# A state-space convolution and a routed expert layer on one core: the convolution's pieces issued in another order up to the second block of scores

## The chip, the core and the metric

The kernel runs on one core of a Trainium2 chip. The core has a matrix engine (TensorE: PE, its weight loads PEld), a vector engine (DVE), an activation engine (ACT), GpSimd (POOL) and a sync engine (SP), on which this kernel issues all its DMAs. Each engine works through its instructions in the order in which they were issued. The metric is the device time of one execution in microseconds, the median of several runs.

## What is computed

Two layers, each behind a layer norm and added to its input; 2048 positions, 512 channels. Cut to what matters:

```python
x = A_u
h = x + conv(layernorm(x))
out = h + peer(layernorm(h))

def conv(u):                       # S4D: a long convolution for each channel
    dt = exp(log_dt); A = -exp(log_A_real) + 1j * A_imag
    C = (C_real + 1j * C_imag) * dt[:, None]
    K = 2 * einsum("dn,dnl->dl", C, exp((A * dt[:, None])[:, :, None] * pos)).real
    return irfft(rfft(u, 2 * L) * rfft(K, 2 * L), 2 * L)[:L] + u * D_skip

def peer(x):                       # 32 heads, 2 x 16 keys, 256 experts
    q = einsum("nd,dhc->nhc", x, w_q)
    i1 = argmax(q[..., :128] @ k1.T); i2 = argmax(q[..., 128:] @ k2.T)
    e = 16 * i1 + i2               # one expert for each head
    act = gelu(einsum("nd,nhd->nh", x, u[e]))
    return einsum("nh,nhd->nd", act, v[e])
```

## The kernel before

The kernel doesn't issue its work where it describes it. It describes 1729 pieces (`plan.add`, line 134: an engine, a function, what it reads, writes and takes), and at the end `plan.run(ORDER)` (line 155) calls their functions in the order of a tuple of numbers, `ORDER` (line 34). The order only decides which instruction stands ahead of which on each engine's queue. What an instruction waits for follows from what it reads and writes, and from the buffers that it takes: seven banks of PSUM shared by nearly all products of the convolution, and rings of two for most tiles in SBUF. A transfer on SP is also a piece of the order, and one that has to wait holds up all transfers behind it. Numbers are given as a piece is described: 0 to 16 are loads, 17 to 64 the parameters, 66 to 112 and 984 to 1102 the projection's pieces, 181 onward the convolution.

The pieces that the order moves:

- **Loads** (line 271): the SSM's parameters (ldt, lar, aim, cre, cim), the keys ka and kb, the input x in eight transfers for the statistics (two tiles, x_105 and x_106 in the rows below), small constants.
- **Parameters** (lines 293 to 436): chains of small operations on ACT and DVE that make the decays' exponents, the roots (lines 332 to 334), angles (line 355, 340 to 342) and magnitudes, for a first part (64 states' columns, 0) and the rest (1). `decays` (line 373) makes eleven powers of the decay with exp: E for the first half of the channels (two calls, 64 and 192 columns), and e1 for the second half (256 columns), which is stored to memory and read back much later (E<-e_d).
- **Projection pieces** (`w_piece(n)`, line 799, n = 0 to 31): w_q times keys is computed on the chip. Each piece is a load of 512 KB (line 822), 16 matmuls (line 828), a copy (832), a transpose (836) and a copy (840); every fourth one is followed by a store to w_d (844). The loads of pieces 2 to 8 go to tiles that are used for something else later (pb, e1, c_s). From piece 11 on each shares a ring of two tiles: its load waits until the matmuls of the piece before the last are through.
- **Statistics and norm** (lines 230 to 262): 64 bn_stats on DVE, then a mean on PE, spread on DVE, square on ACT, parts on DVE, variance on PE, square root on ACT, reciprocal on DVE.
- **The convolution kernel's generation**, 32 rounds i, the heart of the first half: POOL builds magnitudes mg and phases pg (`factors`, lines 538 to 594), ACT the sines and cosines (lines 644 to 647), DVE multiplies (`tables`, lines 651 to 664), PE contracts (`kgen`, line 690: 64 matmuls). mg, pg and the products gf are rings of two. Two rounds give a k tile, copied by ACT and DVE (lines 698 and 702).
- **The transform**, four column blocks c: stage 1 of the normalised input (s1u, line 471, behind the load, subtraction and product of lines 502 to 508) and of k (s1k), stage 2 (line 488), their products (lines 732 to 743, DVE, ACT and POOL), and the first inverse stage (ia, line 764), whose results go to memory. Behind block 3 come the inverse (ib, line 1036), the second norm, scores, selection and experts. That second half starts at about 300 us.

ACT's functions come from tables: where the next one isn't in the table at hand, an ACT_TABLE_LOAD stands ahead. Exp, square root, and sine with arctangent are three tables here.

Of the kernel before, what the change touches and what calls it, by code (L numbers as in the profile page):

```python
# [27 lines left out]
def view(t, off, dims):  # L28
# [6 lines left out]
    0, 18, 19, 2, 5, 1, 4, 71, 3, 66, 87, 11, 76, 81, 92, 17, 20, 21, 22, 6, 24, 25, 23, 27, 30, 26, 29, 35, 36, 37,  # L35
    97, 38, 40, 41, 67, 68, 32, 31, 39, 33, 42, 61, 72, 73, 43, 34, 62, 44, 45, 47, 123, 28, 48, 69, 70, 181, 77, 78,
    74, 46, 54, 79, 55, 88, 89, 82, 83, 80, 84, 93, 94, 95, 102, 8, 75, 984, 59, 90, 98, 91, 108, 49, 64, 56, 184, 99,
    186, 103, 50, 104, 14, 122, 51, 52, 248, 185, 245, 187, 53, 182, 183, 197, 198, 96, 105, 188, 106, 190, 85, 189,
    192, 194, 200, 191, 249, 193, 202, 195, 201, 63, 100, 109, 196, 110, 199, 12, 86, 989, 101, 128, 204, 206, 111,
    203, 215, 129, 207, 205, 112, 57, 58, 208, 218, 220, 222, 985, 986, 987, 990, 216, 217, 988, 209, 16, 991, 992,  # L40
    13, 126, 7, 994, 10, 1000, 227, 228, 246, 116, 229, 387, 993, 219, 125, 124, 995, 996, 224, 230, 997, 998, 127,
    221, 1005, 210, 223, 225, 231, 114, 247, 120, 65, 1001, 1002, 226, 232, 107, 234, 144, 236, 1006, 1010, 211, 212,
    233, 213, 1007, 1003, 1011, 235, 9, 250, 237, 238, 252, 214, 1012, 1004, 239, 1008, 1013, 1015, 117, 1021, 137,
    1009, 254, 256, 121, 115, 240, 118, 119, 253, 243, 1016, 130, 131, 244, 1014, 257, 258, 132, 1017, 1018, 1019,
    388, 261, 262, 251, 264, 266, 133, 138, 1022, 1023, 390, 134, 135, 1026, 1027, 255, 259, 999, 151, 145, 136, 146,
    260, 1028, 1029, 1024, 263, 279, 280, 139, 267, 281, 265, 268, 269, 1030, 147, 1025, 270, 142, 140, 271, 152, 291,
    153, 241, 148, 143, 282, 141, 284, 286, 283, 149, 272, 292, 154, 113, 150, 242, 156, 273, 274, 158, 288, 294, 157,
    155, 159, 285, 160, 277, 289, 1020, 278, 391, 287, 275, 276, 295, 161, 163, 296, 290, 162, 293, 389, 392, 393,
    164, 298, 165, 343, 344, 177, 167, 175, 345, 166, 297, 1031, 299, 300, 394, 301, 302, 168, 357, 178, 358, 359,
    350, 351, 352, 176, 396, 303, 179, 180, 398, 400, 304, 395, 399, 403, 397, 401, 169, 307, 60, 305, 171, 173, 308,  # L50
    306, 319, 406, 408, 404, 407, 170, 174, 454, 172, 348, 346, 320, 349, 405, 421, 410, 402, 422, 423, 1032, 360,
    409, 411, 347, 15, 412, 424, 1033, 413, 433, 362, 1036, 1037, 455, 361, 414, 426, 363, 1038, 1034, 1035, 364, 311,
    434, 315, 451, 415, 428, 425, 1042, 1039, 1040, 593, 1041, 365, 427, 416, 366, 312, 429, 353, 354, 430, 1043,
    1044, 355, 356, 369, 431, 370, 436, 435, 452, 367, 368, 316, 1045, 323, 385, 386, 377, 378, 1047, 1048, 432, 1049,
    437, 438, 324, 440, 549, 563, 439, 550, 317, 318, 551, 1046, 321, 1050, 1051, 371, 372, 373, 374, 379, 313, 322,
    442, 380, 441, 1052, 383, 443, 594, 314, 384, 381, 375, 309, 310, 596, 444, 382, 456, 453, 457, 467, 376, 468,
    458, 460, 459, 462, 552, 597, 553, 554, 463, 555, 570, 339, 464, 335, 340, 445, 461, 331, 465, 470, 446, 472, 474,
    336, 471, 469, 485, 476, 466, 486, 556, 327, 473, 1057, 475, 488, 490, 477, 497, 478, 557, 492, 558, 489, 493,
    325, 337, 328, 333, 479, 480, 487, 491, 332, 571, 494, 498, 500, 326, 564, 338, 502, 504, 506, 495, 501, 598, 499,
    503, 595, 334, 565, 329, 330, 496, 599, 417, 419, 601, 603, 507, 505, 610, 605, 420, 447, 448, 600, 508, 481, 449,  # L60
    611, 612, 418, 661, 602, 606, 509, 510, 607, 604, 608, 513, 483, 511, 609, 450, 482, 613, 484, 514, 572, 658, 629,
    512, 527, 614, 615, 616, 617, 521, 528, 619, 618, 529, 620, 559, 560, 568, 1053, 1054, 522, 621, 569, 1058, 622,
    1059, 517, 530, 623, 1060, 1061, 561, 1055, 575, 573, 566, 518, 562, 628, 631, 632, 633, 641, 576, 635, 574, 630,
    634, 519, 523, 567, 579, 637, 580, 589, 1056, 640, 643, 642, 1063, 756, 770, 1068, 636, 520, 591, 644, 590, 638,
    577, 585, 524, 586, 662, 525, 645, 578, 1064, 646, 639, 647, 1065, 592, 583, 584, 581, 659, 803, 515, 526, 648,
    649, 650, 516, 660, 1066, 1067, 1069, 587, 1070, 1071, 663, 674, 1072, 763, 665, 667, 651, 652, 653, 669, 342,
    341, 1078, 675, 582, 666, 664, 531, 532, 539, 757, 758, 537, 670, 676, 668, 671, 677, 588, 540, 679, 681, 672,
    764, 678, 545, 682, 546, 800, 1073, 683, 680, 684, 673, 759, 761, 685, 538, 692, 695, 697, 699, 686, 693, 694,
    533, 696, 760, 543, 535, 687, 700, 698, 701, 702, 762, 777, 704, 705, 801, 707, 708, 706, 778, 779, 544, 802, 709,
    711, 712, 534, 710, 771, 713, 714, 541, 542, 703, 690, 765, 624, 626, 688, 715, 656, 805, 804, 806, 691, 536, 807,  # L70
    808, 625, 627, 809, 811, 716, 717, 812, 654, 689, 813, 657, 720, 721, 718, 1079, 719, 816, 819, 768, 772, 1080,
    810, 814, 655, 821, 823, 817, 820, 818, 822, 864, 1074, 724, 1075, 726, 1081, 725, 722, 723, 734, 735, 1076, 769,
    1077, 780, 1082, 782, 781, 825, 773, 774, 766, 775, 767, 1084, 1085, 1086, 824, 834, 867, 826, 815, 837, 730, 835,
    727, 731, 836, 1089, 736, 868, 776, 827, 783, 788, 798, 839, 840, 737, 732, 733, 828, 789, 1094, 841, 799, 728,
    729, 790, 791, 786, 787, 838, 796, 797, 784, 843, 794, 785, 795, 847, 548, 547, 742, 844, 865, 846, 848, 849, 744,
    842, 866, 851, 853, 855, 745, 829, 852, 845, 869, 870, 850, 1090, 752, 856, 854, 880, 857, 881, 1091, 871, 1083,
    1099, 873, 875, 872, 876, 753, 858, 748, 877, 743, 883, 749, 738, 874, 878, 898, 859, 885, 887, 1062, 1092, 884,
    792, 879, 793, 888, 889, 882, 886, 750, 890, 899, 740, 739, 910, 891, 1093, 901, 902, 903, 751, 905, 907, 746,
    741, 913, 747, 892, 906, 915, 900, 832, 833, 917, 919, 911, 904, 908, 893, 830, 831, 914, 912, 896, 916, 860, 861,
    862, 918, 909, 920, 921, 863, 922, 894, 897, 923, 926, 895, 927, 924, 925, 1087, 1088, 928, 929, 930, 932, 754,  # L80
    933, 1095, 936, 755, 934, 1096, 1097, 931, 940, 944, 1100, 948, 937, 938, 941, 942, 935, 945, 1098, 1101, 1102,
    952, 956, 939, 949, 943, 953, 946, 947, 950, 951, 954, 957, 958, 955, 1105, 1206, 959, 969, 1103, 1104, 963, 966,
    981, 1207, 1115, 964, 965, 970, 960, 975, 978, 972, 1112, 1119, 1109, 1106, 1120, 967, 1116, 1113, 982, 968, 1107,
    976, 961, 979, 973, 1110, 1121, 971, 1129, 1114, 983, 1108, 1117, 962, 977, 980, 974, 1111, 1130, 1131, 1122,
    1132, 1135, 1133, 1208, 1212, 1118, 1123, 1134, 1136, 1137, 1138, 1139, 1140, 1143, 1213, 1141, 1144, 1145, 1124,
    1214, 1146, 1125, 1126, 1142, 1147, 1281, 1209, 1152, 1210, 1353, 1153, 1163, 1154, 1148, 1149, 1150, 1211, 1215,
    1151, 1155, 1167, 1173, 1156, 1162, 1157, 1158, 1159, 1280, 1279, 1160, 1216, 1352, 1217, 1218, 1164, 1285, 1282,
    1165, 1176, 1283, 1286, 1219, 1166, 1284, 1220, 1161, 1287, 1168, 1169, 1170, 1221, 1354, 1225, 1222, 1288, 1171,
    1226, 1289, 1223, 1227, 1236, 1224, 1290, 1177, 1291, 1228, 1237, 1292, 1127, 1172, 1174, 1178, 1238, 1293, 1175,
    1179, 1184, 1182, 1183, 1239, 1185, 1128, 1294, 1295, 1180, 1186, 1181, 1230, 1231, 1232, 1229, 1309, 1241, 1242,  # L90
    1243, 1240, 1233, 1234, 1296, 1187, 1297, 1235, 1298, 1193, 1195, 1196, 1310, 1190, 1244, 1245, 1189, 1427, 1426,
# [1357 lines left out]
```

## Time and profile before

| | |
|---|---|
| time, median of 3 runs | 501.16 us (500.92 to 502.75) |
| the profiled execution | 502.31 us, span 500.5 us |
| granted clock, mean over the span | 0.988 |
| DMA | 61.04 MB, mean 122 GB/s |
| chain of work that ended last | PE 69%, DVE 19%, ACT 5%, issue 2%, DMA 2%, POOL 1% |

A row of the view of stretches gives, after the range and its length, the busy time of each engine with its count of instructions, the granted clock of TensorE, the DMA share, and GB/s. A row of the timeline gives start and length in us, engine, line, operation, out<-in, shapes, the count, and in brackets the idle time of the engine just ahead and what ended it. "issue" there is idle time for which the profile shows no cause. In the table of the chain it is time in which the engine waited for nothing that the profile shows. DMA rows name the issuing engine as SPq.

### The profile page before, as it was taken

The numbers are of one execution on the slowest core, as the hardware profiler recorded it, in microseconds if no ns is written. First come the engines' busy times: TensorE is split into PE (matmuls) and PEld (weight loads), VectorE is DVE, ScalarE is ACT, GpSimd is POOL, SyncE is SP. The second block draws the span as 40 slices with busy tenths as digits, with TensorE's granted clock in tenths as the row PEclk, the third lists the DMA queues.
The fourth block names the chain that finished last, engine by engine and source line by source line (L and its number), as shares of the span: only waits on it lengthen the run. The fifth ranks groups of instructions, "written<-read, shape, count | busy, mean of one in ns | idle before, by whom it ended". The sixth has DMA issues, their size and how long they took to land.

```text
span 500.5 us, 16696 instructions
## 1 busy us (share of the span) xinstructions
PE 448.6 (90%) x7206; PEld 393.6 (79%) x7206; DVE 408.5 (82%) x708; ACT 300.2 (60%) x596; POOL 325.0 (65%) x344
## 2 busy tenths in 40 slices
PE   0545879999999999999999689999999999999985
PEld 0324669989999989999998688887878888787874
DVE  4879998989988998799775494878979686978994
ACT  4796789986997689966996263454043430416231
POOL 3988997999999999989864303652263516535130
PEclk9999979999999999999999899999999999999999
DMA  7916885354200740045242757320171311010012
GB/s 259 413 52 211 275 297 173 145 156 195 65 3 9 266 131 24 3 102 218 64 162 72 227 158 251 110 103 1 61 226 54 117 56 44 1 45 0 1 51 78
DMA packets 27361, 61.04 MB, mean 122 GB/s; under 512 B 7028, under 2 KB 14456, under 8 KB 26136
## 3 DMA queue, kind: packets, MB, share of 16 engines
q1 hardware_dynamic: 27288, 59.98, 35.3%
q8 instruction: 56, 0.92, 0.8%
q14 instruction: 17, 0.14, 0.1%
HBM read 46.08 MB, written 13.89 MB: 120 GB/s over the span
## 4 chain that ended last, share of the span: by engine, by line
PE 69%; DVE 19%; ACT 5%; issue 2%; DMA 2%; POOL 1%; SPq 0%; ACTq 0%; DVEq 0%
PE sc L1150 14%; PE ia L764 12%; PE s1k L471 6%; PE kps L690 6%; PE s1u L471 5%; DVE oh L1280 5%; PE s2yu L488 5%; PE xu L1157 4%; PE s2yk L488 3%; PE ib L1036 3%; PE o L1327 2%; PE wps L828 2%; PE cnt L1290 2%; DVE U L733 2%; DMA wq<-wq 2%
## 5 line engine op out<-in xcount | busy, mean ns | idle before, releaser
L588 POOL TENSOR_TENSOR mg<-TS 128x1024 f32<-128x1024 f32 x32 | 62.7, 1958 | 11.4 <-PE kps L690 11.1
L557 POOL TENSOR_TENSOR pg<-PS 128x1024 int32<-128x1024 int32 x32 | 68.8, 2152 | 1.0 <-ACT t L644 0.9
L1280 DVE TENSOR_SCALAR oh<-idxb,ec_s 128x2048 bf16<-128x2048 bf16 (+1 forms) x72 | 50.3, 756 | 6.9 <-ACT idxb L1262 6.9
L764 PE MATMUL ia<-ca_s,U 128*128 128x128 f32 x256 | 50.6, 280 | 0.8 <-POOL U L743 0.8
L1192 POOL TENSOR_TENSOR ks<-kq 128x512 f32<-128x512 bf16 x16 | 17.3, 1079 | 49.0 <-DVE kq L1186 48.4
L1060 POOL TENSOR_TENSOR vs<-hc 128x256 f32<-128x256 f32 x8 | 6.3, 789 | 59.7 <-ACT hc L1083 59.7
L645 ACT ACTIVATE t<-t,halfpi 128x512 f32<-128x512 f32 x64 | 42.4, 662 | 2.1
L1150 PE MATMUL sc<-w_hi,hhi 128*128 128x480 f32 x128 | 42.5, 413 | 0.0
L764 PEld LDWEIGHTS ia<-ca_s,U 128*128 128x128 f32 x256 | 39.8, 196 | 1.0 <-POOL U L743 1.0
L644 ACT ACTIVATE t<-pg 128x512 f32<-128x512 int32 x64 | 38.9, 607 | 0.5 <-DVE U L735 0.4
L690 PE MATMUL kps<-mg 128*32 128x64 f32 x1024 | 34.6, 233 | 5.0 <-DVE mg L660 2.8
L764 PE MATMUL ia<-ca_s,yk 128*128 128x128 f32 x192 | 38.0, 280 | 0.6 <-DVE U L735 0.3
L1150 PE MATMUL sc<-w_hi,hlo 128*128 128x480 f32 x128 | 38.4, 381 | 0.0
L1150 PE MATMUL sc<-w_lo,hhi 128*128 128x480 f32 x128 | 38.4, 380 | 0.0
L647 ACT ACTIVATE t<-pg 128x512 f32<-128x512 int32 x64 | 37.9, 608 | 0.3 <-DVE gf L655 0.2
L594 POOL TENSOR_TENSOR mg<-TS 128x512 f32<-128x512 f32 x32 | 37.4, 1172 | 0.1
L690 PE MATMUL kps<-gf 128*32 128x64 f32 x1024 | 34.4, 231 | 0.6 <-issue 0.6
L690 PEld LDWEIGHTS kps<-mg 128*32 128x32 f32 x1024 | 26.0, 117 | 9.2 <-POOL mg L594 4.7
L471 PE MATMUL s1u<-c_s,xs 128*64 128x128 f32 x512 | 33.1, 285 | 0.0
L488 PE MATMUL s2yk<-yk,c_s 128*128 128x128 f32 x256 | 32.6, 279 | 0.4 <-ACT yk L474 0.4
L488 PE MATMUL s2yu<-yu,c_s 128*128 128x128 f32 x256 | 31.9, 279 | 0.1
L471 PE MATMUL s1k<-c_s,k 128*64 128x128 f32 x512 | 31.4, 279 | 0.5 <-DVE k L702 0.5
(200 smaller groups left out, 1385.2 us busy)
## 6 DMA issues: line engine op xcount, KB each, us to landing
wq<-wq SPq DMA_DIRECT2D x25, 512.0 KB, 4.6
t_d<-T SPq DMA_DIRECT2D x24, 256.0 KB, 4.5
Tb<-t_d SPq DMA_DIRECT2D x8, 768.0 KB, 6.6
x<-xa SPq DMA_DIRECT2D x8, 512.0 KB, 6.4
xs<-xb SPq DMA_DIRECT2D x16, 256.0 KB, 3.3
xt<-xt SPq DMA_DIRECT2D x8, 512.0 KB, 4.2
out<-ob SPq DMA_DIRECT2D x7, 512.0 KB, 3.0
c_s<-wq SPq DMA_DIRECT2D x4, 512.0 KB, 10.2
```

What stands on the lines that cost most here:

```text
L471: T.matmul(ps[64 * k:64 * k + 64, g, :], lhs8(4 * n + g), c1_s[:, k], start=True, stop=True)
L488: T.matmul(ps[:, k, :], c2_s[:, kk, :], y[:, :, kk, :], start=True, stop=True)
L557: G.tensor_tensor(view(pg, 0, [[32, 2 * NC], [8, 4], [1, 8]]), view(t["PS"], 1024 + off, [[1, 2 * NC], [128, 4], [0, 8]]), view(t["PS"], 8 ...
L588: G.tensor_tensor(view(mg, 0, [[96, NC], [8, 8], [1, 8]]), view(ts, 512 + 8 * o, [[8, NC], [1, 8], [0, 8]]), view(ts, 8 * o, [[8, NC], [0, ...
L594: G.tensor_tensor(view(mg, 64, [[96, NC], [8, 4], [1, 8]]), view(ts, 1536 + o, [[1, NC], [64, 4], [0, 8]]), view(ts, 1024 + 8 * o, [[8, NC ...
L644: A.activation(p, pg[:, :, k], AF.Abs)
L645: A.activation(p, p, AF.Sin, scale=-SINSCALE, bias=halfpi)
L647: A.activation(p, pg[:, :, k], AF.Sin, scale=SINSCALE)
L690: T.matmul(kps[32 * q:32 * q + 32, 2 * g + h, :], m[:, d, 64:96], m[:, d, 0:64], start=(e == 0), stop=(e == 1))
L764: T.matmul(ps[:, g, :], t[:, 4 * n + g].rearrange("p a b -> p (a b)"), ca_s[:, s, :], start=(s == 0), stop=(s == 1))
L1150: T.matmul(ps[:, 512 * h:512 * h + 480], t[x_][:, q, ts], I[w_][:, q, 480 * h:480 * h + 480], start=(q == 0 and x_ == w_), stop=(q == 3 an ...
L1280: V.tensor_scalar(oh[:, :, 0:ln], t["idxb"][:, :, sl], S["ec"][:, 4 * e + j:4 * e + j + 1], None, op0=ALU.is_equal)
```

## The change

The first 1199 numbers of `ORDER` stand in another order, found by a search with waits for instruction loads counted. They are all pieces of the convolution and of what stands ahead of it, up to the second block of scores; the 530 numbers behind are the same. No piece is added, dropped or altered. ACT has two fewer ACT_TABLE_LOADs, since the table is switched less often. The beginning of the tuple:

```diff
 ORDER = (
-    0, 18, 19, 2, 5, 1, 4, 71, 3, 66, 87, 11, 76, 81, 92, 17, 20, 21, 22, 6, 24, 25, 23, 27, 30, 26, 29, 35, 36, 37,
-    97, 38, 40, 41, 67, 68, 32, 31, 39, 33, 42, 61, 72, 73, 43, 34, 62, 44, 45, 47, 123, 28, 48, 69, 70, 181, 77, 78,
...
+    0, 17, 1, 2, 3, 4, 5, 6, 71, 72, 8, 16, 18, 19, 20, 21, 23, 24, 7, 87, 22, 29, 25, 35, 59, 36, 37, 30, 26, 38, 27,
+    32, 39, 114, 40, 41, 42, 43, 45, 31, 33, 108, 61, 34, 47, 44, 28, 73, 116, 66, 184, 67, 68, 46, 76, 69, 70, 48,
...
```

What this moves is seen in the rows of each engine. First ACT, ahead of the first sine of the convolution kernel (t_0, line 647). E_111 and e_104 are the decays, par, pa and pb parameters, wt and wh the copies of projection pieces. Before, from the second table load of the parameters on:

```order
L840 COPY wh_229<-wps_203 128x120
L373 ACT_TABLE_LOAD
L373 ACTIVATE e_104<-pb 128x256 x11
L840 COPY wh_314<-wps_252 128x120
L832 COPY wt_328<-wps_305 128x128
L832 COPY wt_344<-wps_332 128x128
L840 COPY wh_314<-wps_276 128x120
L647 ACT_TABLE_LOAD
L647 ACTIVATE t_0_386<-pg_378 128x512
```

In the change the decays e_104 stand near the beginning of ACT's queue:

```order
L373 ACTIVATE E_111<-pb 128x64 x11
L373 ACTIVATE e_104<-pb 128x256 x11
L351 ACTIVATE par_101<-pa 128x64
L353 ACTIVATE pb<-pa 128x64
L352 ACTIVATE pa<-pa 128x64
L373 ACTIVATE E_111<-pb 128x192 x11
```

and ahead of the first sine there are only copies:

```order
L840 COPY wh_315<-wps_290 128x120
L832 COPY wt_352<-wps_343 128x128
L832 COPY wt_355<-wps_322 128x128
L840 COPY wh_315<-wps_343 128x120
L832 COPY wt_398<-wps_389 128x128
L647 ACTIVATE t_0_408<-pg_387 128x512
```

The eleven decays moved from right ahead of the first sine to right behind the first part's decays; the two table loads around them are gone.

Second, SP, around the store of the first group of four pieces. Before, behind the last early load of x:

```order
L822 DMA wq_291<-wq 128x1024
L822 DMA c_s<-wq 128x1024
L271 DMA x_106<-xa 128x1024 x2
L844 DMA w_d<-wh_229 512x1x120
L822 DMA wq_463<-wq 128x1024
L271 DMA c_s<-c 128x256
L271 DMA D_81<-dsk 4x128
L271 DMA x_106<-xa 128x1024
```

In the change:

```order
L822 DMA wq_319<-wq 128x1024
L822 DMA c_s<-wq 128x1024 x2
L844 DMA w_d<-wh_248 512x1x120
L822 DMA wq_333<-wq 128x1024
L271 DMA x_106<-xa 128x1024 x2
L822 DMA wq_421<-wq 128x1024
L822 DMA wq_470<-wq 128x1024
L271 DMA x_105<-xa 128x1024
```

The store stands ahead of two loads of x now, and more loads of pieces follow it.

Third, PE, ahead of the first round of kgen (kps_0, line 690). Before:

```order
L836 MATMUL wps_305<-ident,wt_328 128x128
L828 MATMUL wps_416<-c_s,ka_s 32x128 x4
L828 MATMUL wps_416<-c_s,kb_s 32x128 x4
L690 MATMUL kps_0_425<-mg_330 32x64 x4
L690 MATMUL kps_0_425<-gf_392 32x64 x4
```

In the change:

```order
L836 MATMUL wps_412<-ident,wt_424 128x128
L828 MATMUL wps_446<-wq_319,ka_s 32x128 x4
L828 MATMUL wps_446<-wq_319,kb_s 32x128 x4
L836 MATMUL wps_446<-ident,wt_455 128x128
L828 MATMUL wps_473<-wq_421,ka_s 32x128 x4
L828 MATMUL wps_473<-wq_421,kb_s 32x128 x4
L690 MATMUL kps_0_487<-mg_371 32x64 x4
L690 MATMUL kps_0_487<-gf_427 32x64 x4
```

Three more pieces (from tiles wq_333, wq_319 and wq_421) stand on PE ahead of the first kgen.

160 rows, old and new, of the table ORDER are left out of this document.

## The prediction

> **What bounds the kernel now.** First the page's busy line and clock line, then the long stretches by engine.
>
> ```profile
> PE 448.6 (90%) x7206; PEld 393.6 (79%) x7206; DVE 408.5 (82%) x708; ACT 300.2 (60%) x596; POOL 325.0 (65%) x344
> 0.00:37.50 37.50, 11.98 (x152) 7.40 (x152) 26.56 (x69) 25.66 (x75) 27.80 (x44) 1.00 0.66 242
> 37.50:72.00 34.50, 24.39 (x532) 18.72 (x534) 32.33 (x96) 25.46 (x58) 31.69 (x30) 0.95 0.78 268
> 72.00:275.50 203.50, 201.77 (x3838) 189.07 (x3838) 175.87 (x287) 168.64 (x325) 179.86 (x160) 0.99 0.34 113
> 275.50:301.00 25.50, 18.80 (x271) 18.13 (x272) 16.93 (x32) 10.46 (x22) 4.19 (x4) 0.93 0.64 195
> 301.00:500.50 199.50, 191.61 (x2416) 160.28 (x2416) 156.78 (x227) 70.03 (x118) 81.51 (x109) 1.00 0.22 74
> ```
>
> After the range and its length each row holds the busy time of PE, PEld, DVE, ACT and POOL, the granted clock, the DMA share and GB/s. Over the whole span PE is the busiest engine, at 90%. Its missing time stands almost only at the front: 25.5 us of the first 37.5 and 10.1 of the next 34.5, against 1.7 in the 203.5 us that follow. The change ends before the last stretch, whose order is unchanged. So from 72 us on the time is PE's work, which a new order doesn't shorten, and the question is when PE's dense stretch begins. It begins with the first s1u (stage 1 of the normalised input) at 71.91. What stands before it on the path is this:
>
> ```profile
> 31.47 0.27 DVE L334 TENSOR_TENSOR pa<-par,pa 128x112 f32<-128x112 f32 x1
> 33.87 0.69 DVE L651 SCALAR_TENSOR_TENSOR gf<-mg,t 128x512 f32<-128x512 f32 x1 [2.12 <-ACT t L647]
> ...
> 61.84 1.64 DVE L230 BATCH_NORM_STATS2 st<-x 128x6 f32<-128x128 f32 x8
> 64.58 0.22 DVE L243 COPY pc<-mu 128x64 f32<-128x64 f32 x1
> 64.84 0.39 DVE L244 TENSOR_TENSOR pc<-st,pc 128x128 f32<-128x128 f32 x1
> 65.73 0.69 DVE L660 TENSOR_TENSOR mg<-mg,t 128x512 f32<-128x512 f32 x1
> 66.33 0.40 DVE L248 SCALAR_TENSOR_TENSOR dv<-st,pc 128x128 f32<-128x128 f32 x1
> 69.36 0.69 DVE L505 TENSOR_TENSOR xs<-xs,pc 128x512 f32<-128x512 f32 x1 [0.72 <-ACT pc L260]
> 70.08 0.57 DVE L262 RECIPROCAL pc<-pc 128x64 f32<-128x64 f32 x1
> 70.68 1.28 DVE L508 TENSOR_TENSOR xs<-xs,pc 128x512 f32<-128x512 f32 x2
> ```
>
> The columns are start, length, engine, line, operation, operands, count, and the idle time ahead with what ended it. From its first table (L651 at 33.87) DVE works almost without a pause (32.33 of the second stretch's 34.5 us) through tables and statistics until the last statistics end at 63.48. Then mean, spread, square, variance, square root, reciprocal and product follow one another. So **the path to the dense stretch is DVE from its first table on, then the chain of the norm**, and what makes the first table late is a wait of 2.12 us for ACT. ACT's rows:
>
> ```profile
> 26.53 1.28 ACT L373 ACT_TABLE_LOAD   x1
> 27.82 3.48 ACT L373 ACTIVATE e<-pb 128x256 f32<-128x256 f32 x11
> 31.94 1.28 ACT L647 ACT_TABLE_LOAD   x1
> 33.24 0.60 ACT L647 ACTIVATE t<-pg 128x512 f32<-128x512 int32 x1
> ...
> 65.40 0.25 ACT L257 ACTIVATE pc<-pc 128x128 f32<-128x128 f32 x1
> 67.46 0.27 ACT L832 COPY wt<-wps 128x128 f32<-128x128 f32 x1
> 67.75 1.28 ACT L260 ACT_TABLE_LOAD   x1
> 69.04 0.29 ACT L260 ACTIVATE pc<-va,epst 128x64 f32<-128x64 f32 x1
> ```
>
> **The change, part by part.**
>
> *The second half's decays go forward on ACT.* Before, the 11 ACTIVATEs of 3.48 us stand between two ACT_TABLE_LOADs of 1.28 us, right ahead of the first sine. In the change they stand behind the first decays, where the exp table is loaded already. The path loses what held up the sine, and two table loads go: 2 × 1.28 = 2.56 us of ACT's time. What is late next is twofold: POOL's phases
>
> ```profile
> 27.36 4.24 POOL L557 TENSOR_TENSOR pg<-PS 128x1024 int32<-128x1024 int32 x2
> ```
>
> (the first of the two ends at about 27.36 + 2.12 = 29.48), and DVE's last root at 31.47 + 0.27 = 31.74, behind which the first table stands in both orders. So the sine can be early by more than DVE can use, and the gain is DVE's idle time, **2.1 us** (L651 at about 31.75). It is nothing if the sine is held up elsewhere on ACT, where eight copies of the projection's pieces now stand ahead of it, and some 4 us if DVE's roots come earlier too. I take the middle, for which a row exists. On the 3.48 us ahead of the parameters' later ACT steps I put nothing: those then waited for DVE's roots, which wait for DVE itself.
>
> *Turns of the second part go ahead of the first kgen.* L340 to L342 (four operations of 0.62 us, 2.5 us in all) stood behind the tables of kgen 0 and 1 and stand inside those of kgen 0 now. On DVE it is the same work ahead of the last statistics (56 of 64 bn_stats are there in both orders), so it costs the path nothing. Kgen 0 comes 2.1 us earlier and 2.5 us later: as before, at about 38.
>
> *Statistics and norm.* The last statistics end at 63.48 − 2.1 = 61.4. Mean and spread take from 63.48 to 65.23 before, so 63.1 now. Then the square waits: three sine or abs pieces of the tables stand ahead of it on ACT in the change, each of about 0.6 us, of which I charge **1.1 us**. So it runs at 64.4 (65.40 before). Behind it I count what no longer stands in the way: parts (L248) waited 0.6 us behind two table products (square done 65.65, parts 66.33); the reciprocal stood behind a subtraction of 0.69; behind the product two turns of pieces stood ahead of s1u on PE:
>
> ```profile
> 65.89 0.33 PE L836 MATMUL wps<-ident,wt 128*128 128x128 f32 x1 [1.59 <-ACT wt L832]
> 69.43 0.44 PE L690 MATMUL kps<-mg 128*32 128x64 f32 x8 [1.19 <-ACT pc L260]
> 71.29 0.69 PE L836 MATMUL wps<-ident,wt 128*128 128x128 f32 x2
> 71.91 3.47 PE L471 MATMUL s1u<-c_s,xs 128*64 128x128 f32 x30
> ```
>
> (0.6 us). Together 0.6 + 0.7 + 0.6 = 1.9. So s1u begins 2.1 − 1.1 + 1.9 = **2.9 us** earlier, at 69.0. The bounds: 0 if the square waits the rest away, 5 if DVE's roots are early too and nothing waits.
>
> *The clock.* The rows around the norm:
>
> ```profile
> 62.50:68.50 6.00, 3.98 (x69) 2.65 (x65) 5.93 (x16) 5.50 (x13) 5.84 (x7) 1.00 0.95 307
> 68.50:75.50 7.00, 6.07 (x102) 5.60 (x104) 6.21 (x12) 5.54 (x11) 6.77 (x5) 0.51 0.65 271
> ```
>
> After a stretch with PE busy for 66% the clock falls to half for about 7 us. From 71.91 to about 75.4 PE does dense work at half speed, and loses half of it, 1.7 us. The change has about the same matmuls around the norm, 5 us in the 7 to 8 us ahead of s1u, so the window may fall again or not. Between 0 and 1.7 I take **0.8 us**.
>
> In the Trainium skill, "TensorE: Matmul & The Clock Gate", Part 1, the gate falls after an idle window of about 3.4 us. By that rule PE would stay at full clock here, in both orders. The trace disagrees: its longest idle time there is 1.59 us, and the clock fell.
>
> *The dense stretch to the last stage 2.* POOL's last heads and the beginning of the last stage 2 on PE:
>
> ```profile
> 257.37 1.17 POOL L594 TENSOR_TENSOR mg<-TS 128x512 f32<-128x512 f32 x1
> 266.30 2.05 PE L488 MATMUL s2yk<-yk,c_s 128*128 128x128 f32 x16 [0.42 <-ACT yk L474]
> ```
>
> Pieces of the projection change places in it. Counted with the durations of before, PE's work from the first s1u to the last stage 2 is the same within 0.1 us: two pieces that filled holes at its end stand before it now, and two others ahead of s1u. POOL was busy 179.9 of 203.5 us there, and ends at 258.5, 7.8 us before the last stage 2; with s1u 2.9 us earlier some 5 us of that cover are left. A table's factors that come later than before by more than that would show as waits of PE. I put nothing on it.
>
> *The end of the convolution.*
>
> ```profile
> 278.95 0.49 PE L764 MATMUL ia<-ca_s,yu 128*128 128x128 f32 x2 [3.48 <-DVE yu L732]
> 280.29 0.79 PE L764 MATMUL ia<-ca_s,U 128*128 128x128 f32 x2 [0.85 <-POOL U L743]
> ```
>
> PE waits there for DVE's products, so the fillers that left make the wait longer and not the end later: 14.0 us from the last stage 2 to here, in both orders. Nothing, with ±0.5 us for the clock and for loads of the second half that are issued sooner.
>
> *Waits for instruction loads.* The view of waits shows two that I read as such:
>
> ```profile
> PE ib L1036 <- issue: 1.1, 1, 1.1
> PE kps L690 <- issue: 0.6, 1, 0.6
> ```
>
> A new order can hide these 1.7 us or meet others. Between −1.7 and 1.7 I take 0.
>
> *The sum:* 2.9 + 0.8 = 3.7, with 0.1 for PE's work 3.8 us. The profiled execution took 502.31 us (span 500.5), so 498.5 by its measure. It stands 1.15 us above the median of 501.16, against which it is **497.4 us**.
>
> **The rivals.**
>
> *The clock stays at full speed* (the rule cited above, and this kernel's own records from 75 us on): then 1.7 in place of 0.8, 496.5 us. For it speaks that the first s1k products stand between mean and variance now; against it that the window before fell at a similar density. Chance 0.13.
>
> *The front gains more.* DVE's roots are reached 2 us sooner, because the decays' ACTIVATEs and the loads of the parameters go forward; the square doesn't wait (1.1) and the clock stays (0.9 more): 497.4 − 4.0 = 493.4. Against it: POOL was busy 31.69 of 34.5 us in the second stretch, so the tables' factors would have to be early as well. Chance 0.13.
>
> *The gain is eaten by the norm.* ACT is in order, and every table piece ahead of square and root costs 0.6 us. If square and root stand 3 us behind, s1u begins where it did: about 500.5, no change that can be measured. For it: the wait at 69.36 for ACT. Chance 0.20.
>
> *Slower: kgen 0 waits for a load.* In the change kgen 0 stands on PE behind the matmuls of three more pieces, the last of which reads a tile (wq_421) whose load is issued only when the tile's former piece is through. SP's rows of before, the store of the first group, and the loads' sizes and median times to landing:
>
> ```profile
> 34.74 0.64 SPq L844 DMA_DIRECT2D w_d<-wh  x1
> ...
> wq<-wq SPq DMA_DIRECT2D x25, 512.0 KB, 4.6
> c_s<-wq SPq DMA_DIRECT2D x4, 512.0 KB, 10.2
> ```
>
> The store stands at 34.74 in before with nothing behind it issued; in the change the copies that it waits for come some 10 us sooner, so it is issued at about 24.9 and the loads behind it follow. By the order the piece ahead is through on PE at about 32.7, wq_421 is issued then and lands at 37.3 with 4.6 us, just ahead of the tables at 38.3. With the 10.2 us of the loads that share the rings with others it lands at 42.9, kgen 0 is 4.6 us late, and since the tables have two buffers DVE stops behind it: 502.0. If the load ahead of it takes 10.2 us as well (24.9 + 10.2 = 35.1, its matmuls to 36.2), wq_421 lands at 46.4, 8.1 us late: **505.5 us**. It decides from a landing at 38.3 on and makes the kernel slower by over 0.5% from 44.6 (3.8 + 2.5 us behind). For it: the loads of x and of the pieces share the rings in a stretch with a DMA share of 0.78. Chance 0.12.
>
> **How the numbers follow.** The forecast, 497.4, holds from 496 to 499 with a chance of 0.42; the clock's rival (496.5) 0.13; the larger gain (493.4) 0.13; the eaten one (500.5) 0.20; the slower one (505.5) 0.12. A measurement of this kernel can tell about 0.5% from no change, so faster is below 498.65. Below that lie 0.38 of the forecast and the first two rivals, 0.64; within lie the rest of the forecast and nearly all of the eaten gain, 0.23; above, 0.13. The range leaves out the slower rival and the far end of the larger gain: 492.5 to 501.5.
>
> **What the profile of the change would show.** If I am right: the first sine (L647) at about 31.7, with no table load next to the decays of 128x256; DVE's wait of 2.12 at L651 gone; the last statistics done at about 61.4; the square at about 64.4; the first s1u at about 69; the last stage 2 at about 262.5, and the end of the span 3 to 4 us earlier. A wait of kps L690 for a DMA, or of wps L828 for one just ahead of it, shows the slower rival; a square or root long after its operands, with ACT busy on tables, the eaten gain; a granted clock of 1.0 through 62 to 76 us the clock's. I am wrong altogether if PE is no longer dense behind the first s1u: if waits of kps for POOL or DVE, or of "issue", add up to more than 2 us there, or if the end of the convolution takes longer than 14 us.

## The result, and the profile after

| | before | the change |
|---|---|---|
| time, median of 11 runs each, measured side by side | 501.8 us (500.12 to 503.6) | 498.56 us (496.92 to 500.69) |
| ratio to before, 95% interval | | 0.9938, 0.9918 to 0.9958 |
| profiled execution, its span | 502.31 us, 500.5 us | 499.36 us, 497.4 us |
| granted clock, mean over the span | 0.988 | 0.973 |

The kernel is 3.1 us faster (0.62%, 0.42 to 0.82%). The view of stretches of the change, over the same ranges as before (columns as there):

```profile
0.00:37.50 37.50, 14.55 (x240) 8.75 (x243) 30.12 (x75) 26.80 (x84) 28.68 (x48) 0.90 0.83 299
37.50:72.00 34.50, 24.46 (x550) 18.97 (x541) 31.36 (x94) 25.37 (x54) 31.82 (x26) 0.81 0.70 248
72.00:275.50 203.50, 194.47 (x3744) 182.22 (x3742) 176.09 (x287) 164.97 (x320) 180.93 (x162) 1.00 0.34 115
275.50:301.00 25.50, 23.32 (x372) 22.37 (x376) 16.87 (x32) 10.03 (x22) 1.57 (x2) 0.87 0.54 166
301.00:497.40 196.40, 188.03 (x2330) 157.47 (x2318) 154.26 (x224) 69.44 (x117) 81.71 (x109) 1.00 0.21 69
```

The ranges no longer cut the work at the same places: the third now holds the wait behind the last stage 2, which stood in the fourth before. The clock of before's first two ranges (1.00 and 0.95) and with it the mean of 0.988 are read too high, as the last section shows, so these rows aren't compared by it. What answers to the prediction's path is read from the timeline. ACT first, then DVE, then PE:

```profile
8.75 3.47 ACT L373 ACTIVATE e<-pb 128x256 f32<-128x256 f32 x11
28.96 0.60 ACT L647 ACTIVATE t<-pg 128x512 f32<-128x512 int32 x1 [0.88 <-POOL pg L557]
63.03 0.24 ACT L257 ACTIVATE pc<-pc 128x128 f32<-128x128 f32 x1
66.22 0.29 ACT L260 ACTIVATE pc<-va,epst 128x64 f32<-128x64 f32 x1
```

```profile
30.04 0.27 DVE L334 TENSOR_TENSOR pa<-par,pa 128x112 f32<-128x112 f32 x1
30.23 0.68 DVE L651 SCALAR_TENSOR_TENSOR gf<-mg,t 128x512 f32<-128x512 f32 x1
...
43.28 1.64 DVE L230 BATCH_NORM_STATS2 st<-x 128x6 f32<-128x128 f32 x8 [1.72 <-DMA x<-xa]
...
58.46 2.41 DVE L230 BATCH_NORM_STATS2 st<-x 128x6 f32<-128x128 f32 x12
61.97 0.22 DVE L243 COPY pc<-mu 128x64 f32<-128x64 f32 x1
63.30 0.38 DVE L248 SCALAR_TENSOR_TENSOR dv<-st,pc 128x128 f32<-128x128 f32 x1
66.55 0.57 DVE L262 RECIPROCAL pc<-pc 128x64 f32<-128x64 f32 x1 [0.47 <-ACT pc L260]
67.15 0.69 DVE L508 TENSOR_TENSOR xs<-xs,pc 128x512 f32<-128x512 f32 x1
```

```profile
67.98 4.12 PE L471 MATMUL s1u<-c_s,xs 128*64 128x128 f32 x64 [0.66 <-DVE xs L508]
...
163.61 0.43 PE L828 MATMUL wps<-wq,ka_s 128*32 128x128 f32 x8 [1.43 <-DMA wq<-wq]
180.75 0.42 PE L828 MATMUL wps<-wq,kb_s 128*32 128x128 f32 x5 [0.64 <-issue]
224.78 1.16 PE L488 MATMUL s2yk<-yk,c_s 128*128 128x128 f32 x8 [0.72 <-DVE U L735]
263.32 7.41 PE L488 MATMUL s2yk<-yk,c_s 128*128 128x128 f32 x64 [0.43 <-ACT yk L474]
275.96 0.80 PE L764 MATMUL ia<-ca_s,yu 128*128 128x128 f32 x2 [5.23 <-DVE yu L732]
```

The first sine waits 0.88 us for POOL's phases and for nothing on ACT; DVE goes from its last root to its first table without a pause. The twelve statistics that start at 58.46 end the last at 60.87. So the chain runs as forecast, each step a little earlier than that:

| point (start, where nothing else is said) | before | the change | earlier |
|---|---|---|---|
| first table on DVE | 33.87 | 30.23 | 3.64 |
| last statistics, end | 63.48 | 60.87 | 2.61 |
| square | 65.40 | 63.03 | 2.37 |
| square root | 69.04 | 66.22 | 2.82 |
| first s1u | 71.91 | 67.98 | 3.93 |
| last stage 2 | 266.30 | 263.32 | 2.98 |
| first products of the last block's ia | 278.95 | 275.96 | 2.99 |

The gain is made by the first s1u, and a part of it is lost in the dense stretch. From the first s1u to the last stage 2 it is 194.4 us before and 195.3 in the change. PE's waits there are 1.6 us before (0.61 "issue", 0.27, 0.33, 0.42) and 4.1 in the change (the four above with 0.16, 0.43, 0.28 for DVE and ACT): 2.5 more. PE's work there is 1.5 us shorter, since its first products aren't done at half clock. 3.9 + 1.5 − 2.5 = 2.9. In a second profile of the change (below) the same stretch takes 193.9 us, with 2.6 us of waits, so of the loss 1.0 us is in both profiles and 1.5 in the first alone.

### The profile page after: what moved, and what is told of

Same layout as the page of the kernel before. It is cut to its first block, busy times and chain, and to the rows that moved or that the text cites. A ratio compares the mean times of both kernels' runs of the same rounds, so it can differ in the third digit from the quotient of the medians.

```text
span 497.4 us, 16692 instructions
## 1 busy us (share of the span) xinstructions
PE 444.8 (89%) x7206; PEld 389.8 (78%) x7206; DVE 408.7 (82%) x708; ACT 296.6 (60%) x594; POOL 324.7 (65%) x344
## 4 chain that ended last, share of the span: by engine, by line
PE 66%; DVE 21%; ACT 4%; DMA 3%; POOL 3%; issue 2%; SPq 0%; DVEq 0%; ACTq 0%; POOLq 0%
PE sc L1150 14%; PE ia L764 12%; PE s2yu L488 6%; PE kps L690 5%; DVE oh L1280 5%; PE s1k L471 4%; PE xu L1157 4%; PE s1u L471 4%; PE s2yk L488 3%; PE ib L1036 3%; DMA wq<-wq 2%; PE o L1327 2%; PE cnt L1290 2%; PE wps L828 2%; DVE U L733 2%
## 5 line engine op out<-in xcount | busy, mean ns | idle before, releaser
L828 PE MATMUL wps<-wq,ka_s 128*32 128x128 f32 x200 | 12.4, 326 | 25.1 <-DMA wq<-wq 22.0
L690 PE MATMUL kps<-mg 128*32 128x64 f32 x1024 | 33.5, 229 | 1.0 <-DVE mg L660 0.7
L690 PE MATMUL kps<-gf 128*32 128x64 f32 x1024 | 32.9, 226 | 0.0
L471 PE MATMUL s1u<-c_s,xs 128*64 128x128 f32 x512 | 31.8, 276 | 1.1 <-DVE xs L508 0.7
L488 PEld LDWEIGHTS s2yk<-yk,c_s 128*128 128x128 f32 x256 | 30.2, 192 | 3.1 <-ACT yk L474 1.3
```

The costliest lines, as they stand in the source:

```text
L471: T.matmul(ps[64 * k:64 * k + 64, g, :], lhs8(4 * n + g), c1_s[:, k], start=True, stop=True)
L488: T.matmul(ps[:, k, :], c2_s[:, kk, :], y[:, :, kk, :], start=True, stop=True)
L690: T.matmul(kps[32 * q:32 * q + 32, 2 * g + h, :], m[:, d, 64:96], m[:, d, 0:64], start=(e == 0), stop=(e == 1))
```

## Experiments

Two theories stood against each other. **The front:** all of the gain comes from the order up to the first s1u. **The rest:** it comes from the order behind, for which waits for instruction loads had been counted. Inside the front it was open which of the terms of the sum carries it. Each kernel is a new order of the same pieces; what a change of `ORDER` does is said in words, with a line or two of the tuple.

### The two halves of the order

Up to the first s1u the change's numbers and then what is left in before's order (a cut behind the 274th number), and the other way round (behind the 279th of before). The line of the first kernel's tuple in which the cut falls, against the change:

```diff
-    244, 266, 257, 134, 213, 260, 135, 390, 136, 263, 139, 142, 151, 267, 152, 153, 265, 145, 214, 268, 143, 279, 140,
+    244, 266, 257, 134, 213, 260, 135, 390, 136, 263, 139, 214, 388, 151, 145, 146, 279, 280, 267, 281, 265, 268, 269,
...
```

> The changed order up to the first s1u, before's order for all the rest. Theory 'the front': the first s1u at about 68 (71.9 before, 68.0 in the change) with the clock at full speed, none of the new waits of the change's dense stretch, so the last stage 2 begins some 5 us earlier than before (about 261) and the kernel takes some 5 us less than before. Rival 'the rest': the gain of the change comes from the order behind the first s1u, and this kernel gives back what it gained by the last stage 2: less than 1.5 us faster than before.

> Before's order up to the first s1u, the changed order for the rest. Theory 'the front': the first s1u at about 72 with the clock at half behind it, the change's waits in the dense stretch (a load of a piece 1.4 us, a product 0.7) come on top: 0 to 3 us slower than before. Rival 'the rest': 2 to 3 us faster than before, as the change is.

Measured: 0.9946 (0.9918 to 0.9975) for the front alone, 1.0077 (1.0048 to 1.0106) for the rest alone. The front's kernel, first s1u and last stage 2 on PE:

```profile
68.57 2.89 PE L471 MATMUL s1u<-c_s,xs 128*64 128x128 f32 x48 [1.72 <-DVE xs L508]
...
261.62 2.05 PE L488 MATMUL s2yk<-yk,c_s 128*128 128x128 f32 x16 [0.41 <-ACT yk L474]
```

The same two of the rest's kernel:

```profile
74.30 3.88 PE L471 MATMUL s1u<-c_s,xs 128*64 128x128 f32 x64
...
267.78 7.41 PE L488 MATMUL s2yk<-yk,c_s 128*128 128x128 f32 x64 [0.42 <-ACT yk L474]
```

With the front alone the last stage 2 stands at 261.62, 4.7 us ahead of before and 1.7 ahead of the change; the distance between its two rows is 193.05 us, without the change's wait for a load. It isn't quite the same work: the matmuls of two pieces (32 of L828), which the change has ahead of the last stage 2, stand behind it here as in before, and PE is busy for 190.1 us of the distance in place of 191.0. With the rest alone the last stage 2 stands at 267.78, 1.5 us behind before. Its first s1u stands at 74.30 because a product of s1k and a piece come first there, so the distance between its rows, 193.5 us, doesn't tell what the rest's order costs. So the front carries the gain, and the new order of the rest costs where the front is the old one; by which of its moves isn't shown. The front alone is 2.7 us faster than before, not 5 as expected, and no better than the change: what it is ahead at 261.62 it partly loses behind. From the last stage 2 to the first matmul that both tuples have at the same index (the second block of scores) it takes 56.65 us, and 55.99 in the change.

Both kernels of the new front were taken again with five rounds, to see whether the front alone beats the change:

> The changed kernel again, beside the next two on the same chip. Both theories on the clock expect the same order of waits and a first s1u at 67.9 to 69.6; theory 'the window decides' expects the half clock to fall elsewhere among the first 75 us than in the first profile, where it stood at 29.9 to 40.1 and 47.0 to 57.2, and the first s1u to move with it; the rival 'the order decides' expects the same stretches.

> The changed order up to the first s1u, before's order behind it, with more rounds. Theory 'the rest costs': the change's order behind the first s1u is some 1 to 2 us slower than before's (195.3 us from the first s1u to the last stage 2, 193.0 here), so this kernel is 0.5 to 1.5 us faster than the change. Rival 'the rest is even': within 0.5 us of the change.

Measured: 0.9932 (0.9909 to 0.9954) for the change, 0.9938 (0.9914 to 0.9962) for the front alone. They can't be told apart. On the clock neither expectation came true: the stretches at half clock fall elsewhere in the second profile (last section), but the first s1u moves by 0.16 us only. In these two profiles the distance from the first s1u to the last stage 2 is 193.9 us for the change (67.82 to 261.72) and 192.9 for the front alone (69.64 to 262.55), and behind it to the second block of scores 56.17 and 57.97. There the front's kernel waits longer for "issue". The view of waits, of the change's second profile first:

```profile
PE ib L1036 <- issue: 0.5, 1, 0.5
```

```profile
PE ib L1036 <- issue: 1.6, 2, 1.0
```

The distance is 1.0 us shorter with the old order because of the two pieces that stand behind it there: PE is busy for 189.9 us of it in place of 191.0, and its waits are the same (2.7 and 2.6 us). What this wins is paid back behind, 1.1 of 1.8 us in waits that I read as instruction loads. That reading rests on the name "issue" alone.

### The decays, alone and undone

Before's order with the decays of 128x256 moved to behind the first ones, and the product that they need moved ahead of the second step on DVE:

```diff
-    0, 18, 19, 2, 5, 1, 4, 71, 3, 66, 87, 11, 76, 81, 92, 17, 20, 21, 22, 6, 24, 25, 23, 27, 30, 26, 29, 35, 36, 37,
+    0, 18, 19, 2, 5, 1, 4, 71, 3, 66, 87, 11, 76, 81, 92, 17, 20, 21, 22, 6, 24, 29, 25, 23, 27, 30, 26, 35, 59, 36,
...
```

> Before's order with two pieces moved: the second part's exponent (one product on DVE) ahead of the second step, and the eleven decays of 128x256 right behind the first decays on ACT, with two table loads fewer. Theory 'decays': the first sine no longer waits for ACT; DVE's idle time of 2.1 us ahead of its first table goes, the last statistics end at about 61.4 (63.5 before) and the first s1u begins about 2 us earlier; 1.5 to 3 us faster than before. Rival 'another wait is late': the sine is early, but kgen or the statistics wait for loads behind the store on SP, and the first s1u begins within 0.7 us of before's 71.9: no change.

Measured: 0.999 (0.9971 to 1.001): no change that can be told. ACT and DVE of this kernel:

```profile
9.68 1.72 ACT L373 ACTIVATE E<-pb 128x64 f32<-128x64 f32 x11 [2.12 <-DVE pb L359]
11.30 3.46 ACT L373 ACTIVATE e<-pb 128x256 f32<-128x256 f32 x11
23.67 0.53 ACT L354 ACTIVATE par<-par 128x448 f32<-128x448 f32 x1 [2.10 <-DVE pa L334]
```

```profile
33.24 0.27 DVE L334 TENSOR_TENSOR pa<-par,pa 128x112 f32<-128x112 f32 x1
33.43 0.68 DVE L651 SCALAR_TENSOR_TENSOR gf<-mg,t 128x512 f32<-128x512 f32 x1
```

The first sine is 1.9 us earlier (31.30), and DVE's wait for it is gone, as expected. But the 3.5 us of decays now stand ahead of the parameters' later steps on ACT, the roots on DVE end at 33.51 in place of 31.74, and the first table is only 0.4 us earlier. The first s1u starts at 71.04, 0.9 us early. Then the opposite, the change with the decays put back ahead of the first sine:

```diff
-    109, 110, 185, 197, 187, 199, 111, 188, 112, 985, 994, 57, 986, 987, 189, 190, 192, 58, 191, 246, 193, 990, 991,
+    110, 185, 197, 187, 199, 111, 59, 188, 112, 985, 994, 57, 986, 987, 189, 190, 192, 58, 191, 246, 193, 990, 991,
```

> The changed order with the eleven decays of 128x256 put back right ahead of the first sine on ACT, as before had them, with the two table loads around them. Theory 'decays': the first sine 5 us later than in the change (about 34), DVE's first table 4 us later (about 34.5), the last statistics 2.7 us later since 1.7 us of the change's early tables were lost to a wait for x, the first s1u at about 70.7: 2 to 3 us slower than the change. Rival 'the loads and roots': the decays were never on the path, since the rest of the opening sets the first table; the first s1u within 1 us of the change's 68.0.

Measured: 1.0037 (1.0014 to 1.0061) of before, where the change has 0.9938. Its ACT:

```profile
28.91 1.28 ACT L373 ACT_TABLE_LOAD   x1
30.20 3.48 ACT L373 ACTIVATE e<-pb 128x256 f32<-128x256 f32 x11
33.70 1.28 ACT L647 ACT_TABLE_LOAD   x1
34.99 0.60 ACT L647 ACTIVATE t<-pg 128x512 f32<-128x512 int32 x1
```

The first sine is 6.0 us later than in the change, the first table 5.4 (35.63), the last statistics 4.9 (65.76), and the first s1u 4.9 (72.87). Nearly all of it arrives: the wait for x of 1.72 us, by which I expected a part to be swallowed, did not swallow it: it is still there, with 1.61 us. So the decays are on the path in the new front, worth more than the whole gain, and worth nothing that the runs can tell in the old one, where the roots come 1.8 us later with them.

### The opening alone, and the end of the norm alone

The change's order up to the first table (the cut is behind the 125th number), before's behind it:

> The changed order up to the first table of the first round (the parameters, the first loads, the decays moved forward), before's order for all the rest. Theory 'the opening': DVE's first table starts at about 30.3 (33.9 before, 30.2 in the change) and most of it arrives at the first s1u: 69 to 70 (71.9 before), and the kernel is 2 to 3 us faster than before. Rival 'statistics and norm': the earlier tables run into waits for x and for the projection's loads, and the first s1u begins at 71 or later; under 1 us.

Measured: 1.0048 (1.0029 to 1.0066), slower than before. DVE of this kernel, and PE's first kgen:

```profile
30.30 0.68 DVE L651 SCALAR_TENSOR_TENSOR gf<-mg,t 128x512 f32<-128x512 f32 x1
30.89 0.68 DVE L652 TENSOR_TENSOR gf<-mg,t 128x512 f32<-128x512 f32 x1
36.73 1.64 DVE L230 BATCH_NORM_STATS2 st<-x 128x6 f32<-128x128 f32 x8 [5.16 <-DMA x<-xa]
```

```profile
40.90 0.44 PE L690 MATMUL kps<-mg 128*32 128x64 f32 x8 [9.37 <-DVE mg L664]
```

The first table is where the change has it, and then DVE stands for 5.16 us in front of statistics on a part of x that before had loaded first and the change's opening loads later. The kernel tells nothing for or against the opening; it tells that the order of the x loads on SP and that of the statistics on DVE belong together.

Before's order with only the end of the norm as in the change:

```diff
-    388, 261, 262, 251, 264, 266, 133, 138, 1022, 1023, 390, 134, 135, 1026, 1027, 255, 259, 999, 151, 145, 136, 146,
-    260, 1028, 1029, 1024, 263, 279, 280, 139, 267, 281, 265, 268, 269, 1030, 147, 1025, 270, 142, 140, 271, 152, 291,
+    388, 261, 262, 251, 264, 266, 133, 138, 1022, 1023, 390, 134, 135, 1026, 1027, 255, 259, 999, 151, 136, 139, 145,
+    146, 260, 142, 140, 1028, 263, 279, 280, 267, 281, 265, 268, 269, 1029, 1030, 1024, 147, 1025, 270, 271, 152, 291,
```

> Before's order with only the end of the norm as the change has it: the reciprocal ahead of the second tile's subtraction, then the first tile's product, the first s1u right behind kgen 4, and the two turns of pieces behind it. Theory 'terms add': the first s1u 1.1 to 1.3 us earlier than before (70.6 to 70.8) with all ahead of it as before, and the last stage 2 as much earlier. Rival 'given back': PE's next products wait for DVE instead, and the last stage 2 begins within 0.3 us of before's 266.3.

Measured: 1.0051 (1.0032 to 1.0069), slower. From the square root to the first s1u it takes 2.25 us (70.52 to 72.77) in place of 2.87, so 0.6 of the expected 1.1 to 1.3 is there; but from the first s1u to the last stage 2 it takes 195.7 us in place of 194.4, with new waits of PE for ACT of 1.10 and 0.38 at 79.2 and 77.1. It is given back within eight microseconds, as the rival said. All of the norm also came 1.5 us later than in before in this profile: kgen 3 began 1.5 us later, and the statistics waited for its copy. The edit begins behind kgen 3 in the order, so this delay isn't shown to be its doing; without it the profile accounts for 0.7 us (1.3 lost, 0.6 won), and the rest of the 0.5% stays open.

### Waits in the dense stretch, and the fillers at its end

The change with the piece whose load PE waits for at 163.6 put later on PE:

```diff
-    756, 635, 636, 621, 637, 1065, 529, 342, 527, 566, 567, 1066, 1067, 638, 622, 573, 574, 1074, 517, 528, 661, 530,
-    515, 569, 1075, 583, 523, 640, 662, 641, 642, 659, 584, 518, 643, 645, 623, 644, 585, 586, 524, 591, 592, 579,
+    756, 635, 636, 621, 637, 1065, 529, 342, 527, 566, 567, 1066, 1067, 638, 622, 573, 574, 517, 528, 661, 530, 515,
+    1074, 1075, 569, 583, 523, 640, 662, 641, 642, 659, 584, 518, 643, 645, 623, 644, 585, 586, 524, 591, 592, 579,
```

> The changed order with one piece's matmuls (the piece whose load PE waits for at 163.6, 1.43 us) put some four products of stage 2 later on PE. Theory 'waits in the dense stretch cost their length': that wait is gone, the last stage 2 begins 1.4 us earlier relative to the first s1u (195.3 us between them in the change, 193.9 here). Rival 'POOL or DVE sets the pace there': kgen 18 and 20 begin when they did, and the distance stays within 0.4 us of 195.3.

Measured: 0.9945 (0.9922 to 0.9968). The wait for the load is gone and one of 0.87 us for ACT stands near it (166.6); from the first s1u to the last stage 2 it takes 194.8 us, 0.5 less than in the change's first profile and 0.9 more than in its second. In that second profile, of the same kernel, little is left of the wait for this load:

```profile
162.24 0.43 PE L828 MATMUL wps<-wq,ka_s 128*32 128x128 f32 x8 [0.23 <-DMA wq<-wq]
```

In the kernel with the decays put back, where this part of the order is the change's, it is 0.72 us. So most of the 1.43 us was one execution's, and neither theory holds as it was put: the move is worth nothing that can be told.

The change with its last two pieces put back between the products of the last stage 2:

```diff
...
-    897, 894, 918, 919, 862, 830, 832, 916, 920, 831, 921, 833, 922, 863, 755, 923, 860, 924, 861, 895, 926, 925,
-    1097, 927, 932, 928, 936, 1098, 1104, 933, 934, 944, 929, 937, 935, 945, 930, 931, 938, 939, 946, 947, 940, 941,
+    916, 920, 831, 921, 833, 922, 863, 755, 923, 860, 924, 861, 895, 926, 925, 927, 932, 928, 1095, 1096, 936, 1097,
+    1098, 933, 934, 944, 929, 937, 935, 945, 930, 931, 938, 939, 946, 947, 940, 1100, 1101, 941, 754, 942, 943, 1105,
...
```

> The changed order with the last two pieces of the projection (their matmuls, transposes, copies and the store behind them) put back between the products of the last stage 2, as before had them. Theory 'PE sets the stretch': the last stage 2 begins 1.7 to 1.9 us earlier than in the change (about 261.5), PE's wait behind it is 3.5 us as before and not 5.2, the half clock behind it is shorter: 1.8 to 2.7 us faster than the change. Rival 'the loads': the store and the weights' loads behind it come 10 us later, the evictions or the inverse wait for them, and the gain is under 0.7 us.

Measured: 1.0022 (1.0003 to 1.004), slower than the change by about 4 us. ACT and DVE of this kernel tell why:

```profile
266.36 0.27 ACT L832 COPY wt<-wps 128x128 f32<-128x128 f32 x1 [2.75 <-PE wps L828]
267.52 0.26 ACT L840 COPY wh<-wpt 128x120 f32<-128x120 f32 x1 [0.90 <-PE wpt L836]
267.81 1.07 ACT L739 COPY ki<-s2yk 64x512 f32<-64x512 f32 x2
```

```profile
268.42 0.69 DVE L732 TENSOR_TENSOR yu<-s2yk,U 128x512 f32<-128x512 f32 x1 [7.46 <-ACT ki L739]
```

My edit set the pieces' copies ahead of ACT's first copy of the last products. ACT waits 2.75 us for a matmul of the piece, and DVE's chain of products, which sets the end of the convolution, starts 4.8 us behind the last stage 2 (263.66) in place of 1.8. The experiment doesn't answer its question; what it shows is the price of two copies of 0.27 us at the wrong place of a queue: 3 us.

### The seam a little later

The seam is the place where the front's kernel goes over from the change's order to before's. Here it lies behind the 306th number.

> The same with the seam a little later, behind the sixth round of kgen, so that the first s1u's are those for which the change's norm ends (the first tile first). Theory: PE's waits of 1.72 and 0.70 us at the seam of the former kernel shrink to 0.7 in all, the last stage 2 begins some 1.5 us earlier, at about 260; 1 to 2.5 us faster than the change. Rival: DVE and POOL set the pace behind the seam, and what PE gains there is waited for by kgen 7; no faster than the former kernel.

Measured: 0.9957 (0.9939 to 0.9976), no faster than the kernels above. No profile of it can be read, so why the later seam doesn't help stays open. None of the kernels beats the change beyond the intervals.

## Why the prediction was right, point by point

**The second half's decays.** The wait of 2.12 us is gone and the table loads with it. What is late next on ACT's side is POOL's phases, as forecast (0.88 us of wait). The term was put at 2.1 us by before's roots, and was 3.6: the roots themselves end at 30.31 in place of 31.74. This is the upper bound that the term had named ("some 4 us if DVE's roots come earlier too"). The reason given for 2.1 was mistaken in one place: I had put nothing on the 3.48 us that now stand ahead of the parameters' later steps on ACT, since those waited for DVE. The experiment with the decays alone shows that they cost: its roots come 1.8 us later. The change avoids it by the other moves of its opening: its first decays begin at 7.14 us, 1.8 ahead of before's, and e1 follows at 8.75 at once, where in that experiment it starts at 11.30.

**Turns ahead of kgen 0.** Forecast at about 38, no earlier than before; it is 36.57. Right in that it didn't matter.

**Statistics and norm.** Of the 3.64 us, 2.61 arrive at the last statistics; 1.72 us of DVE's idle time for x stand between. The square's wait was charged 1.1 us and is 0.24 (2.16 us from the last statistics' end to the square, 1.92 before). What was to be gained behind the square, 1.9 us, is 1.56 (3.93 − 2.37). So the sum of 2.9 is 3.9: the first two terms were sized too cautiously, the third too high by 0.3.

**The clock.** The term stood at 0.8 between 0 and 1.7. Behind the first s1u the clock is full in the change, and PE's work is 1.5 us shorter. That was the rival "the clock stays at full speed" (496.5), to which the forecast gave 0.13. The windows behind the first s1u in before and in the change:

```profile
71.90:75.40 3.50, 3.50 (x35) 3.49 (x36) 3.50 (x7) 2.19 (x6) 3.50 (x3) 0.51 0.39 162
```

```profile
68.00:75.00 7.00, 6.84 (x145) 6.00 (x149) 6.90 (x12) 6.92 (x13) 6.76 (x8) 1.00 0.40 110
```

In all seven profiles with the change's norm the clock is full by the first s1u, give or take 0.1 us; in the five with before's norm (one of them with the change's end of it) it is at half for some stretch from 69 us on (0.50, 0.51, 0.83 and 0.92 on average in windows behind their first s1u, or up to 73.9 where the first s1u came at 74.30). That the order has a part in it is what this suggests, since the half clock begins at another time in each execution; it is not shown, nor is the move that would do it. The change has two more s1k products between mean and square root, and the longest wait of PE there is 1.02 us against 1.59. The rule cited from the Trainium skill, that the clock falls after about 3.4 us without work, gave the right outcome for the change's first profile. It gave the wrong one for before, where the longest wait ahead of the fall is 1.59 us, and for the change's second profile, where the clock is at half around 62.8 to 66.0 us behind waits of 1.15 us at most since 48 us.

**The dense stretch.** Put at 0.1 gain, it was 2.5 us of waits: the step of the prediction that failed. What I had counted was PE's work, which is the same, and POOL's cover, which held (POOL's waits for kgen are 9.1 us, 11.1 before). What I had not counted is that pieces in a new order meet their operands elsewhere. Of the 4.1 us of waits 1.43 was for a load's landing (0.23 in the second profile), 0.64 "issue" (0.37), the rest for DVE and ACT, the same in both. So the loss is 2.5 us in the first profile and 1.0 in the second. The bound named for it, 2 us of waits of kps for POOL or DVE or of "issue", was not reached: kps waits for neither there and "issue" is 0.64. With the waits of all PE's work for DVE (0.16 + 0.43 + 0.72) it would be 1.95, just under it.

**The end of the convolution.** 12.6 us from the last stage 2 to the first product of ia in both kernels, PE's wait 5.23 in place of 3.48, as forecast: the fillers that left made the wait longer and not the end later.

**Instruction loads.** 1.7 us of "issue" behind 72 us before, 1.0 in the change; taken as 0.

**The rivals.** The slower one did not come: the last piece ahead of kgen 0 started at 35.11, behind ACT's copy and not behind its load, and kgen 0 waited 0.38 us for POOL. The eaten gain did not come either, since the square waited 0.24 us. The larger gain came in part: the roots were early (1.4 us, not 2), the square hardly waited and the clock stayed, but the dense stretch took 2.6 us of it back.

So 3.8 us were forecast and 3.1 measured, by a front that gains 1.7 us more than forecast (1.0 in the chain, 0.7 by the clock) and a dense stretch that gives 2.6 back. The mechanism of the front was right; that the number came so near is luck, since the two errors, 1.7 and 2.6 us, have opposite signs.

## What to carry to other kernels

Where in-order queues are tuned against each other, a good order is worth what all its moves make together: the three small parts tried here gave, each alone, 0.1% faster to 0.5% slower, and the whole 0.6% faster. To find what a reorder does, cut it by time rather than by part: one order up to a point and the other behind it told at once which half carried the gain. Such a kernel meets waits at the cut or behind it that neither order has (1.72 us in the front's kernel, 5.16 in the opening's), so these are looked for before its time is read. And count, for each piece that is moved, the small copies that go with it on every in-order queue: 0.5 us of copies ahead of a chain's first step cost 3 us here.

## What the runs showed of the hardware

The clock's record of the same kernel differs between executions. Windows of the change from 62.8 us on, first and second profile; the number ahead of the last two is the granted clock:

```profile
62.80:66.00 3.20, 2.69 (x36) 2.11 (x36) 3.11 (x6) 2.82 (x6) 3.12 (x4) 1.00 0.02 10
```

```profile
62.80:66.00 3.20, 3.20 (x26) 2.75 (x24) 2.73 (x5) 2.44 (x4) 3.12 (x3) 0.50 0.10 41
```

The trace's stretches of half and full clock are multiples of 3.41 us (3.41, 6.83, 10.24 and up to 27.3 at half, in twelve profiles), begun at another time in each execution.

The granted clock of a range can mislead. The trace of before has no entry of the clock ahead of 58.29 us, that of the change none ahead of 23.06, and the views count as full what has no entry. The matmuls tell more. A range of before, then eight matmuls of kgen in it, and eight behind 58.29:

```profile
37.90:40.00 2.10, 2.02 (x65) 1.88 (x65) 2.10 (x7) 2.07 (x6) 0.93 (x2) 1.00 0.94 311
38.17 0.47 PE L690 MATMUL kps<-gf 128*32 128x64 f32 x8
60.11 0.29 PE L690 MATMUL kps<-gf 128*32 128x64 f32 x8
```

In the change the same eight take 0.47 us where the record says half:

```profile
36.75 0.47 PE L690 MATMUL kps<-gf 128*32 128x64 f32 x8
```

So before ran at half clock there, although the view says 1.00. An estimate by the matmuls' lengths and the records: of the first 72 us some 62 were at half clock in before and some 44 in the change. How much the front gains by that isn't shown; the two profiles of the change differ in these stretches, and their first s1u by 0.16 us.
